# Float64 weights turned into float32 by shifting the scaled upper word: three VectorE and one ScalarE operation a piece

## The chip, the cores and the metric

The kernel runs on one core of a Trainium2 chip. The metric is the device time of one execution in microseconds, which includes the little that lies around the program's first and last instruction. Three runs of the kernel before the change took 480.67, 481.02 and 481.49 us.

The engines are called here as the profile calls them: PE (TensorE, the matrix engine), DVE (VectorE), ACT (ScalarE), POOL (GpSimd) and SP (SyncE, which issues all the DMAs of this kernel). Each engine takes its instructions strictly in the order in which the program gives them; an instruction that waits for another engine's semaphore holds up everything behind it on its own engine.

## The reference, cut to what matters

The first half is an mLSTM cell over 4 batches, 8 heads, 768 steps and a head width of 40; the second is a feed-forward block with an exact GELU over the 3072 rows that the cell gives.

```python
for t in range(S):
    m_new = np.maximum(f_gate[:, :, t] + m, i_gate[:, :, t])
    f_stab = np.exp(f_gate[:, :, t] + m - m_new)
    i_stab = np.exp(i_gate[:, :, t] - m_new)
    C = f_stab * C + i_stab * np.einsum('bhd,bhe->bhde', vt, kt)
    n = f_stab * n + i_stab * kt
    h_tilde = np.einsum('bhde,bhe->bhd', C, qt)
    y[:, :, t] = sigmoid(o_gate[:, :, t]) * h_tilde / np.maximum(np.abs(n . qt), 1.0)
x = y as (3072, 320)
h = x @ w_in                                    # 320 x 2048
g = 0.5 * h * (1.0 + erf(h / sqrt(2)))
out = g @ w_out                                 # 2048 x 320
```

All inputs are float32 but the two weights: `randn(...).astype(float32)` is multiplied by a numpy float64 scalar, and the products `w_in` and `w_out` are float64. [...]

## The kernel before, in words

**The cell.** The 768 steps are cut into six chunks of 128 (`NCH`), and each chunk into the four batches. A chunk's part of the cell is done with matrix products: for each batch the transposes of q and k (line 481), the scores (L507), the product of the scores with the decay weights on DVE (L510; the weights themselves are ACT's exponentials, L432, eight a batch), the products with the values (L621), the new state (L545, L550, ACT's copies at L560 for the first chunk), the division by the denominator on DVE (`finish`, L634 to L645) and the transposes of y (L656).

**The feed-forward block.** It follows chunk by chunk: `up_step` for the first chunk (L761, L767, GELU at L771), `first_down_steps` (L868), and for the five other chunks products of split parts (`up`, L816 and L827, GELU at L831) and seven products in place of eight (`down_steps`, L891).

**The weights.** They are fetched in 26 `pieces`: ten of 128 partitions by 512 weights for `w_in` (eight `w_in` and two `w_rest`), then 16 of 128 by 320 for `w_out`. `fetch` (L336) issues the DMAs of one piece from SP into one of four buffers `bits`, in which each weight's lower word `lo` lies ahead of its upper word `hi`, so that both are read at a stride of two words. `conv_one` and `conv_two` make the float32 from it:

* `conv_one`: DVE takes the exponent's bits out of `hi` (L357), ACT turns them into a power of two in two operations (L359, L360), and meanwhile DVE takes the mantissa's bits out of `hi` (L362) and adds the lower word (L364).
* `conv_two`: DVE puts the sign on the power of two (L371), multiplies the two parts (L374), and the next piece but three is fetched.

So a piece takes five operations of DVE and two of ACT. In `conv_one` nothing on DVE reads what ACT makes; the first reader of it is L371, in `conv_two`.

**The order.** Nothing is scheduled by a tool: `tc.manual_schedule()` keeps each engine's instructions in the order in which the Python code gives them, and the strings `FRONT` (first two chunks) and `DOWN` (the others) write this order down by hand, one letter a step. `K` is the next piece's `conv_one`, `J` the next piece's `conv_two`; w is the weights of the decay, s the scores, v the products with the values, y `finish`, x the transposes of y, c the carry of the state; capitals are the second chunk; `A` and `U` are steps of the first up product, `F` of the first down product. The letters `I` and `k` give a number of matrix products whose results are not read (L386, L215). The part of `FRONT` in which the first pieces lie is:

```python
O1 K L2 Q s0 O3 w2 q D k2 d P3 t1 w3 c0 L3 J v0 t2 K K y0 s1 I7 v1
I8 O2 J g1 L4 I5 c1 K I1 I2 y1 s2 x0 t3 B4 O4 B5 g2 J x1 s3 v2 c2 L5 y2 H T0 x2 G0 v3 g3 c3 K y3 M1 J L6 J A x3
```

Of the kernel before, what the change touches and what calls it, by code (L numbers as in the profile page):

```python
# [9 lines left out]
F32 = mybir.dt.float32  # L10
F32R = mybir.dt.float32r
BF16 = mybir.dt.bfloat16
U32 = mybir.dt.uint32
AF = mybir.ActivationFunctionType
OP = mybir.AluOpType

P = 128

I23 = 2.0 ** 23
PART = 1.0 - 2.0 ** -13  # L20
BASE = 1.0 + 2.0 ** -12

# [15 lines left out]
def kernel(  # L40
# [16 lines left out]
    nc = tc.nc  # L57
# [17 lines left out]
    WP = 512  # L75
# [3 lines left out]
    const = ctx.enter_context(tc.tile_pool(name="const", bufs=1))  # L79
    wts = ctx.enter_context(tc.tile_pool(name="wts", bufs=NW))  # L80
    raw = ctx.enter_context(tc.tile_pool(name="raw", bufs=2))
# [13 lines left out]

    w_out = const.tile([P, NF, DM], F32, name="w_out")
    ident = const.tile([P, P], F32, name="ident")
    e_hi = const.tile([P, 1], F32, name="e_hi")
    e_lo = const.tile([P, 1], F32, name="e_lo")
    first_x = raw.tile([P, NX + 1, TG], F32, name="first_x", tag="x", bufs=1)  # L100
    aT = const.tile([P, NCH, BH], F32, name="aT")
# [110 lines left out]
    def warm(n):  # L212
        cold = ps_h.tile([P, P], F32, name="cold", tag="h")
        for _ in range(n):
            nc.tensor.matmul(cold, w_out[:, 0, 0:P], w_out[:, 0, 0:P], start=True, stop=True, skip_group_check=True)  # L215

    nc.vector.memset(w_out[:, 0, 0:P], 0.5)
    warm(6)
    nc.vector.memset(e_hi, 1151.0 * I23)
    nc.vector.memset(e_lo, 255.0 * I23)  # L220

    nc.scalar.activation(out=m0[:, 1:2], in_=e_lo[0:BH], func=AF.Exp, scale=0.0)
# [92 lines left out]
    pieces = []  # L315
# [15 lines left out]
        return w_all[i // 4 * 5 + (2 if x == NX else x + (i % 4) // 2 * 3)]  # L331
    for f in range(NF):
        pieces.append(([w_src["out"][f * P:(f + 1) * P, :]], w_out[:, f, :]))
    bits, sig, pow2 = {}, {}, {}

    def fetch(i):  # L336
        if i >= len(pieces):
            return
        src, dst = pieces[i]
        n = sum(x.shape[0] * x.shape[1] for x in src) // (2 * P)  # L340
        bits[i] = raw.tile([P, WP, 2], U32, name="bits", tag="bits", bufs=NB)[:, 0:n, :]
        to = bits[i].rearrange("p n two -> p (n two)")
        row = col = 0
        for x in src:
            nc.sync.dma_start(out=to[row:row + x.shape[0], col:col + x.shape[1]], in_=x)
            row, col = (row + x.shape[0]) % P, col + (x.shape[1] if x.shape[0] == P else 0)

    def conv_one(i):

        if i < len(pieces):  # L350
            n = bits[i].shape[1]
            lo, hi = bits[i][:, :, 0], bits[i][:, :, 1]
            s = sig[i] = raw.tile([P, WP], F32, name="sig", tag="sig")[:, 0:n]
            p = pow2[i] = raw.tile([P, WP], F32, name="pow", tag="pow")[:, 0:n]
            su, pu = s.bitcast(U32), p.bitcast(U32)

            nc.vector.tensor_scalar(out=pu, in0=hi, scalar1=20, scalar2=0x7FF,  # L357
                                    op0=OP.logical_shift_right, op1=OP.bitwise_and)
            nc.scalar.activation(out=p, in_=pu, func=AF.Relu, scale=-I23, bias=e_hi)  # L359
            nc.scalar.activation(out=pu, in_=p, func=AF.Relu, scale=-1.0, bias=e_lo)  # L360

            nc.vector.tensor_scalar(out=su, in0=hi, scalar1=0xFFFFF, scalar2=0x100000,  # L362
                                    op0=OP.bitwise_and, op1=OP.bitwise_or)
            nc.vector.scalar_tensor_tensor(out=s, in0=lo, scalar=2.0 ** -32, in1=su, op0=OP.mult, op1=OP.add)  # L364

    def conv_two(i):

        if i < len(pieces):
            hi, p = bits.pop(i)[:, :, 1], pow2.pop(i)
            pu = p.bitcast(U32)  # L370
            nc.vector.scalar_tensor_tensor(out=pu, in0=hi, scalar=0x80000000, in1=pu,  # L371
                                           op0=OP.bitwise_and, op1=OP.bitwise_or)
            dst, s = pieces[i][1], sig.pop(i)
            nc.vector.scalar_tensor_tensor(out=dst, in0=s, scalar=2.0 ** -20, in1=p, op0=OP.mult, op1=OP.mult)  # L374
            fetch(i + NB)


# [14 lines left out]
    class Cell:  # L392
# [278 lines left out]
        def split_x(self, b):  # L671
            px, t = self.px.pop(b), slice(b * L, (b + 1) * L)
            hi = parts["x"][:, :, t]
            nc.vector.scalar_tensor_tensor(out=parts["x_lo"][:, :, t], in0=px, scalar=-1.0 / BASE, in1=hi, op0=OP.mult, op1=OP.add)
            nc.vector.tensor_tensor(out=parts["x_all"][:, :, t], in0=px, in1=hi, op=OP.subtract)
# [24 lines left out]
    def split_weight():  # L700
# [12 lines left out]
        w_lo.append(w_f(F32R, "w_in_lo"))  # L713
        nc.vector.scalar_tensor_tensor(out=w_lo[i], in0=w_hi[i], scalar=-BASE * 2.0 ** 12, in1=w, op0=OP.mult, op1=OP.add)

# [240 lines left out]
    def cell_steps(c, letters, before=None):  # L956
# [11 lines left out]
                 d=lambda: decays_last(0, 1), q=lambda: decays_last(1, NCH - 1), r=halves_out, p=halves_back,  # L968
                 A=in_turn(first_up_steps(0)), U=in_turn(first_up_steps(1)), F=in_turn(first_down_steps(first_g)),
                 K=in_turn(lambda i=i: conv_one(i) for i in n_pieces), H=products_begin,  # L970
                 J=in_turn(lambda i=i: conv_two(i) for i in n_pieces), Z=split_weight)
    steps |= cell_steps(0, "mwgtscvyx") | cell_steps(1, "MWGTSCVYXR")
    play(FRONT, steps)
# [40 lines left out]
```

## Time and profile before

| | |
|---|---|
| runs | 480.67, 481.02, 481.49 us (median 481.02) |
| profiled execution | span 479.0 us from the first to the last instruction; its own device time is not listed apart from the three runs, whose median is 2.0 us above the span |
| granted TensorE clock | 1.000 over the whole span |
| PE, DVE, ACT, POOL busy | 470.5, 351.5, 222.2, 70.4 us |
| conversion of the weights on DVE | 26 pieces between 14.2 and 125.6 us |
| the same on ACT | 26 pieces between 16.9 and 124.2 us |
| PE's last long wait | before 46.6 us; from there the chain that ended last runs on PE, with short exceptions, to the end |

How to read it: the profile gives each instruction's start and duration; an instruction that follows another on DVE or ACT without a wait may start some 0.1 us before the end of the one ahead of it. A matrix product of float32 stands in the trace as two instructions. The times in the text are microseconds from the first instruction. The releaser behind an arrow in square brackets is the instruction that ended an engine's idle time.

### The profile page before, as it was taken

How to read it: one execution, taken by the hardware profiler on the slowest of the kernel's cores; microseconds unless marked ns; L12 is line 12 of the kernel's file. 1: busy time of each engine (PE TensorE's matmuls, PEld its weight loads, DVE VectorE, ACT ScalarE, POOL GpSimd, SP SyncE). 2: the span in 40 equal slices, each digit the busy share in tenths (PEclk: the TensorE clock that was granted, in tenths of full speed). 3: DMA queues.
4: the chain of work that ended last, by engine and by line, in shares of the span. 5: the costliest groups of instructions: out<-in, count | busy, mean ns of one | idle time of the engine just before them, and what ended most of it. 6: DMA issues, size and time to landing. Idle time of an engine off the chain costs nothing.

```text
span 479.0 us, 11954 instructions
## 1 busy us (share of the span) xinstructions
PE 470.5 (98%) x4740; PEld 410.1 (86%) x4740; DVE 351.5 (73%) x762; ACT 222.2 (46%) x477; POOL 70.4 (15%) x104
## 2 busy tenths in 40 slices
PE   7899999999999999999999999999999999999997
PEld 7787888877777999977999977999977999977997
DVE  7899789798879999847589846589756599624321
ACT  6986999944532942112952113952113952112300
POOL 3001210000020225200324200324100222000000
PEclk9999999999999999999999999999999999999999
DMA  9998966289420367541356551367641350100001
GB/s 171 197 210 191 192 175 152 64 203 194 139 30 4 38 109 181 79 98 12 40 114 154 80 111 14 39 109 172 102 79 12 42 89 3 55 1 0 1 1 55
DMA packets 170423, 44.49 MB, mean 93 GB/s; under 512 B 156448, under 2 KB 163904, under 8 KB 170368
## 3 DMA queue, kind: packets, MB, share of 16 engines
q1 hardware_dynamic: 170368, 43.73, 46.4%
q8 instruction: 37, 0.61, 0.5%
q14 instruction: 18, 0.15, 0.1%
HBM read 39.58 MB, written 4.13 MB: 91 GB/s over the span
## 4 chain that ended last, share of the span: by engine, by line
PE 78%; issue 10%; DVE 7%; SPq 2%; DMA 1%; ACT 1%; POOL 0%; DVEq 0%; POOLq 0%
PE po L891 27%; PE pu L816 19%; PE po L868 7%; PE pu L761 5%; PE pu L827 5%; PE ph L621 4%; PE ps L523 2%; PE pu L767 1%; PE pf L589 1%; SPq L147 1%; PE px L656 1%; PE pf L578 1%; PE ps L507 1%; SPq L157 1%; PE pt L481 1%
## 5 line engine op out<-in xcount | busy, mean ns | idle before, releaser
L891 PE MATMUL po<-w_out,g 128*128 128x160 f32 x640 | 91.6, 301 | 0.0
L891 PEld LDWEIGHTS po<-w_out,g 128*128 128x128 f32 x640 | 87.7, 190 | 2.0 <-ACT g L831 1.8
L831 ACT ACTIVATE g<-pu 128x512 f32<-128x512 f32 x80 | 40.8, 614 | 52.9 <-PE pu L827 52.8
L891 PE MATMUL po<-w_sums,sums 128*128 128x160 f32 x320 | 47.7, 303 | 0.0
L891 PEld LDWEIGHTS po<-w_sums,sums 128*128 128x128 f32 x320 | 44.1, 190 | 0.7
L816 PE MATMUL pu<-x_hi,w_in_hi 128*128 128x512 f32 x160 | 41.7, 402 | 0.0
L666 ACT ACTIVATE x_hi<-px 128x384 fp32r<-128x384 f32 x20 | 9.8, 489 | 67.0 <-PE px L656 67.0
L816 PE MATMUL pu<-x_lo,w_in_lo 128*128 128x512 f32 x160 | 40.6, 395 | 0.0
L432 ACT ACTIVATE W<-W,aT 128x128 f32<-128x128 f32 x128 | 39.2, 388 | 0.1
L816 PEld LDWEIGHTS pu<-x_hi,w_in_hi 128*128 128x128 f32 x160 | 28.5, 188 | 9.3 <-ACT g L831 4.1
L748 DVE TENSOR_TENSOR sums<-g 128x512 f32<-128x512 f32 x20 | 13.8, 688 | 30.8 <-ACT g L831 30.8
L816 PEld LDWEIGHTS pu<-x_lo,w_in_lo 128*128 128x128 f32 x160 | 30.1, 188 | 7.2
L868 PE MATMUL po<-w_out,g 128*128 128x320 f32 x128 | 35.2, 433 | 0.0
L868 PEld LDWEIGHTS po<-w_out,g 128*128 128x128 f32 x128 | 24.0, 190 | 9.5
L831 ACT ACT_TABLE_LOAD x5 | 6.4, 1283 | 55.1 <-DMA blocks<-in_k_dram 27.6
L720 DVE TENSOR_TENSOR w_in_mid<-w_in_hi,w_in_lo 128x512 fp32r<-128x512 f32 x20 | 13.8, 688 | 24.4 <-PE pu L816 24.4
L816 PE MATMUL pu<-x_all,w_mid 128*128 128x512 f32 x80 | 31.6, 395 | 0.0
L816 PE MATMUL pu<-x_all,w_in_mid 128*128 128x512 f32 x80 | 31.6, 395 | 0.0
L444 POOL MEMSET g<- 32x1024 f32 x8 | 7.6, 945 | 150.1 <-ACT W L432 124.5
L406 POOL TENSOR_SCALAR_AFFINE_SELECT W<-W 128x1024 f32<-128x1024 f32 (+2 forms) x20 | 21.3, 1076 | 54.8 <-DMA W<-M_d 42.2
L904 DVE TENSOR_TENSOR o_sb<-po,o_sb 128x320 f32<-128x320 f32 (+1 forms) x27 | 12.5, 464 | 22.8 <-PE po L891 18.8
L761 PE MATMUL pu<-first_x,w_in 128*128 128x256 f32 x128 | 29.1, 382 | 0.1
(183 smaller groups left out, 915.6 us busy)
## 6 DMA issues: line engine op xcount, KB each, us to landing
W<-M_d SPq DMA_DIRECT2D x16, 512.0 KB, 5.6
bits<-in_moe_w_in_dram SPq DMA_DIRECT2D x20, 256.0 KB, 4.6
bits<-in_moe_w_out_dram SPq DMA_DIRECT2D x16, 320.0 KB, 3.3
ob<-in_o_gate_dram SPq DMA_DIRECT2D x24, 160.0 KB, 3.5
out_dram<-o_sb SPq DMA_DIRECT2D x24, 160.0 KB, 2.1
vb<-in_v_dram SPq DMA_DIRECT2D x14, 160.0 KB, 5.1
kb<-in_k_dram SPq DMA_DIRECT2D x14, 160.0 KB, 5.1
g<-M_d SPq DMA_DIRECT2D x4, 512.0 KB, 4.4
```

The source lines that it names most:

```text
L406: nc.gpsimd.affine_select(out=x, in_=x, compare_op=OP.is_ge, fill=1.0e30, base=base, pattern=[[0, H], [1, x.shape[2]]], channel_multiplier=-1)
L432: nc.scalar.activation(out=W[n][:, h, :], in_=src, func=AF.Exp, scale=-1.0, bias=aT[:, self.c, r:r + 1])
L621: nc.tensor.matmul(ph[r, h, :], Pm[:, h, r], vb[turn_of(n)][:, h, :], start=True, stop=True)
L720: nc.vector.tensor_tensor(out=w_mid[i], in0=w_hi[i], in1=w_lo[i], op=OP.add)
L748: nc.vector.tensor_tensor(out=s1, in0=a21, in1=a22, op=OP.add)
L761: nc.tensor.matmul(banks[-1][e][:, i - i0, :], in_tile(i, x)[:, e, i % 2 * P:(i % 2 + 1) * P], first_x[:, x, t0:t1], start=(x == 0 and i = ...
L816: nc.tensor.matmul(pus[i][e], w[k][:, e, i * P:(i + 1) * P], x[:, k, :], start=(n == 0 and k == 0), stop=False, skip_group_check=True)
L827: nc.tensor.matmul(pu[e], w[r, i // 2, i % 2 * P:(i % 2 + 1) * P], x[r, NX, :], start=False, stop=(n == 2), skip_group_check=True)
L831: nc.scalar.activation(out=g.t[:, HF * e + i, :], in_=pu[e], func=AF.Gelu, scale=4097.0)
L868: nc.tensor.matmul(po[b], g.t[:, f, b * L:(b + 1) * L], w_out[:, f, :], start=(f == 0), stop=(f == NF - 1))
L891: nc.tensor.matmul(bank[at][:, i, :], lhs(j, t), rhs(j), start=(first and i == 0 and j == 0), stop=(i == n - 1 and j == HF - 1), skip_grou ...
L904: nc.vector.tensor_tensor(out=to, in0=pb, in1=x, op=OP.add)
```

## The change

`conv_one` and `conv_two` make the float32 in another way. The upper word is read as if it were a float32, whose exponent has eight bits; a product with 2^-112 takes 112 off that exponent, that is 896 = 1023 - 127 off the eleven bits. Shifted to the left by three, the word then is a float32 without its sign and without its three lowest bits. These are the lower word times 2^-29, rounded, and the sign is the top bit of the upper word.

* ACT multiplies the upper words by 2^-112 in place (one operation in `conv_one`, strided in and out).
* DVE turns the lower words into the three bits in place (one operation in `conv_one`).
* DVE merges the sign of the upper word, as ACT left it, and the three bits into the weight's tile (the third operation of `conv_one`).
* DVE shifts the upper words by three and merges them with the weight's tile (the only operation of `conv_two`).

The tiles `sig`, `pow` and `e_hi` go. The order of the steps in `FRONT` stays, and so do the DMAs and their order.

```diff
+NEAR = 0.9374
-    e_hi = const.tile([P, 1], F32, name="e_hi")
-    nc.vector.memset(e_hi, 1151.0 * I23)
-    bits, sig, pow2 = {}, {}, {}
+    bits = {}
 def conv_one(i):
     if i < len(pieces):
-            n = bits[i].shape[1]
             lo, hi = bits[i][:, :, 0], bits[i][:, :, 1]
-            s = sig[i] = raw.tile([P, WP], F32, name="sig", tag="sig")[:, 0:n]
-            p = pow2[i] = raw.tile([P, WP], F32, name="pow", tag="pow")[:, 0:n]
-            su, pu = s.bitcast(U32), p.bitcast(U32)
-
-            nc.vector.tensor_scalar(out=pu, in0=hi, scalar1=20, scalar2=0x7FF,
-                                    op0=OP.logical_shift_right, op1=OP.bitwise_and)
-            nc.scalar.activation(out=p, in_=pu, func=AF.Relu, scale=-I23, bias=e_hi)
-            nc.scalar.activation(out=pu, in_=p, func=AF.Relu, scale=-1.0, bias=e_lo)
-
-            nc.vector.tensor_scalar(out=su, in0=hi, scalar1=0xFFFFF, scalar2=0x100000,
-                                    op0=OP.bitwise_and, op1=OP.bitwise_or)
-            nc.vector.scalar_tensor_tensor(out=s, in0=lo, scalar=2.0 ** -32, in1=su, op0=OP.mult, op1=OP.add)
+            dst = pieces[i][1].bitcast(U32)
+
+            nc.scalar.activation(out=hi.bitcast(F32), in_=hi.bitcast(F32), func=AF.Copy, scale=2.0 ** -112)
+            nc.vector.tensor_scalar(out=lo, in0=lo, scalar1=NEAR * 2.0 ** -29, scalar2=None, op0=OP.mult)
+            nc.vector.scalar_tensor_tensor(out=dst, in0=hi, scalar=0x80000000, in1=lo, op0=OP.bitwise_and, op1=OP.bitwise_or)

 def conv_two(i):
     if i < len(pieces):
-            hi, p = bits.pop(i)[:, :, 1], pow2.pop(i)
-            pu = p.bitcast(U32)
-            nc.vector.scalar_tensor_tensor(out=pu, in0=hi, scalar=0x80000000, in1=pu,
-                                           op0=OP.bitwise_and, op1=OP.bitwise_or)
-            dst, s = pieces[i][1], sig.pop(i)
-            nc.vector.scalar_tensor_tensor(out=dst, in0=s, scalar=2.0 ** -20, in1=p, op0=OP.mult, op1=OP.mult)
+            hi = bits.pop(i)[:, :, 1]
+            dst = pieces[i][1].bitcast(U32)
+            nc.vector.scalar_tensor_tensor(out=dst, in0=hi, scalar=3, in1=dst, op0=OP.logical_shift_left, op1=OP.bitwise_or)
             fetch(i + NB)
```

## The prediction

> **What bounds the kernel now.** I read the page first (engines, slices), then busy time by stretch, then the chain of waits, and last the time lines of DVE and ACT beside each other.
>
> ```profile
> span 479.0 us, 11954 instructions
> PE 470.5 (98%) x4740; PEld 410.1 (86%) x4740; DVE 351.5 (73%) x762; ACT 222.2 (46%) x477; POOL 70.4 (15%) x104
> ...
> PE   7899999999999999999999999999999999999997
> ```
>
> Busy time by stretch (start:end, length, then PE, PEld, DVE, ACT, POOL, granted clock, DMA share, GB/s):
>
> ```profile
> 12.00:24.00 12.00, 10.76 (x137) 8.51 (x135) 10.39 (x28) 11.69 (x40) 0.00 (x0) 1.00 1.03 197
> 24.00:36.00 12.00, 11.38 (x159) 10.00 (x158) 10.98 (x26) 9.66 (x17) 0.00 (x0) 1.00 1.03 210
> 36.00:48.00 12.00, 11.19 (x131) 9.16 (x128) 11.59 (x28) 8.44 (x17) 2.39 (x2) 1.00 0.85 190
> 48.00:93.60 45.60, 45.60 (x508) 39.53 (x506) 37.22 (x85) 43.73 (x83) 4.86 (x4) 1.00 0.65 150
> ```
>
> From 48 us PE has no idle time; the chain runs on it from 46.59 to the end. Only what moves the start of that run, or opens a hole in it, moves the time. Before 48, PE, DVE and ACT take turns: PE is idle 1.24 + 0.62 + 0.81 = 2.67 us in the three stretches. So work taken off DVE can gain some 2.7 us at most, while a late product moves everything behind it. The pieces' place, DVE first, then ACT:
>
> ```profile
> 14.24 0.41 DVE L357 TENSOR_SCALAR pow<-bits 128x512 uint32<-128x512 uint32 x1
> ...
> 15.02 0.69 DVE L364 SCALAR_TENSOR_TENSOR sig<-bits,sig 128x512 f32<-128x512 uint32 x1
> 15.63 0.25 DVE L234 COPY ewT<-pg 128x96 f32<-128x96 f32 x1
> ...
> 21.67 0.42 DVE L357 TENSOR_SCALAR pow<-bits 128x512 uint32<-128x512 uint32 x1
> ...
> 24.57 0.49 DVE L634 TENSOR_TENSOR ob<-ph,ob 128x320 f32<-128x320 f32 x1
> ...
> 29.21 0.42 DVE L357 TENSOR_SCALAR pow<-bits 128x512 uint32<-128x512 uint32 x1
> ```
>
> ```profile
> 14.89 2.09 ACT L432 ACTIVATE W<-pm,aT 128x128 f32<-128x128 f32 x8
> 16.89 0.71 ACT L359 ACTIVATE pow<-pow,e_hi 128x512 f32<-128x512 uint32 x1
> ...
> 24.84 0.73 ACT L359 ACTIVATE pow<-pow,e_hi 128x512 f32<-128x512 uint32 x1
> ...
> 31.25 0.72 ACT L359 ACTIVATE pow<-pow,e_hi 128x512 f32<-128x512 uint32 x1
> ```
>
> The reader should lay these two side by side. DVE starts piece 0 at 14.24, ACT at 16.89; piece 1 at 21.67 and 24.84; piece 3 at 29.21 and 31.25; further down the same lists piece 4 at 39.67 and 41.59, piece 6 at 47.85 and 52.11, piece 7 at 54.57 and 59.63, piece 11 at 73.96 and 77.46. ACT lags because eight exponentials, table loads or copies of PE's results stand ahead of its part. Before, nobody pays: DVE reads ACT's result only in the later step `conv_two` (5.1 us of waits in all, 3.0 of them one).
>
> **The change part by part.** *DVE work.* A piece loses one two-constant operation (L362, 0.42 us at 512 columns, 0.32 at 320) and one with two tensors (0.69, 0.49): 10 x 1.11 + 16 x 0.81 = 24.1 us. What is left is priced by its like: the scaling of the lower words by L357 (0.42, 0.32; uint32 and stride two as there, but its output is strided and its arithmetic not bitwise, so up to L364's 0.69 and 0.49), both merges by L371 (0.69, 0.49).
>
> *ACT work.* Two operations (0.72 + 0.72; 0.56 + 0.56) become one. It is a Copy with a constant scale and no bias tile like L712 (median 0.62 at 512), so I take 0.62, and 0.47 at 320 (L438, 0.46, is near); the bounds are 0.59 (L484) and, as no row shows stride two in place on ACT, the 1.44 of both operations that it replaces; DVE's L364 reads at stride two at the 0.69 of L374's dense operands, so I stay near the dense price. That saves 8 + 10 = 18 us of ACT. L712's Copy stands between exponentials and GELU without a table load, and the built program has 32 loads as before.
>
> *The new wait.* The third operation of `conv_one`, the merge of the sign, reads the upper word that ACT has just scaled. In the built program it waits on ACT's semaphore. So DVE now stops inside `conv_one` until ACT has come to the piece; queued behind it on DVE are `finish`, the score products (L510), the values' weighting and the state update, for which PE and then ACT wait. I walked the queues with the profile's durations, each instruction at the later of its queue and its inputs:
>
> 1. Piece 0: ACT is free at 16.90 (its exponentials wait for nothing new) and done at 17.52. DVE is ready at 14.66, so it stalls 2.9; the merge ends at 18.25 and L234 starts at 18.17, not 15.63: +2.54. L510 had idled 0.58 for PE at 16.66, so it is +1.88, and PE, which had waited 0.41 for DVE's decays (L282), is +1.74.
> 2. Piece 1: `conv_two` of piece 0 is 0.72 shorter; DVE starts at 21.67 + 1.74 - 0.72 = 22.7 and is ready at 23.1. ACT's own queue moved with PE: 24.84 + 1.74, done at 27.24. Stall 4.2. Piece 2 follows without one; L634 starts at 28.96, not 24.57: +4.39, and PE's values product, which waited for L510, goes from 27.61 to 32.00.
> 3. Piece 3: ACT's copies of the state (L560, 30.64 + 4.39) stand ahead, ACT is done at 36.16, DVE stalls 3.0; L634 30.61 becomes 36.81. Idle time on PE and one shorter `conv_two` take back 0.7: the first up product, 40.80, is +5.49.
> 4. Piece 4: ACT done at 47.60, stall 2.1; then two `conv_two` save 1.4. The second up product, 46.59, is +5.74.
> 5. Pieces 5 to 9: stalls of 0.6, 3.25, 2.5, 2.4, one of none; PE has enough queued, nothing is added.
> 6. Pieces 10 and 11: ACT is behind its GELU and tables; stalls of 3.3 and 1.0 make the state update (L565, 76.05) late, and L545 at 78.06 waits 1.15 more: +6.89. After that the walk finds no new hole in PE's run: the pieces of `w_out` stay ahead of the products that read them.
>
> *SP.* `conv_two` still issues the fetch four pieces on, and SP already stands 30.6 us before such issues; these and the loads behind them slide with the rest. A piece lands in 4.6 us and has over ten (piece 8: issued 44.5, used 62.9), so I cost it at nothing; without that cover one late piece costs its landing. POOL gets no work. The tiles `sig` and `pow` go, and with them waits of L720's tiles past 129 us, where PE has no idle time before them: nothing. One memset of 0.06 us goes: nothing.
>
> *Sum.* The walk gives 479.0 + 6.9 = 485.9 for this execution, and the median of the runs stands 2.0 above its span: 487.9. In the walk L639 and L645 keep their 0.75 and 0.99 us at 42.10 and 42.88, beside two operations of POOL (0.49 and 0.23 elsewhere); moved away from them the path loses 1.0. I take half: 487.4.
>
> [...] The row: in the first 14 pieces ACT starts its part 0.5 to 5.2 us after DVE. [...] With the scaling on DVE (10 x 0.42 + 16 x 0.32 = 9.3 us of the 24.1 given back) the wait would go, and the sum would be that of the first rival below.
>
> **The rivals.** *The wait is covered, and the time falls.* If ACT reached its part before DVE reaches the merge, 1.1 us less DVE work in a piece would bring the first up products forward. The chain of waits passes through conversion at 23.1, 39.8 and 43.9, which speaks for it. PE's idle time bounds it by 2.7; half of that gives 479.7. It decides where ACT's start in a piece lies no later than DVE's; the lists have it later in all of the first 14 pieces, by 0.5 to 5.2 us, which speaks against it.
>
> *PE's covered run takes it all up, no change.* Step 5 shows stalls that cost nothing. But steps 1 to 4 lie where PE already waits on DVE and ACT. Time 481.
>
> *The operations are dearer too.* In the walk ACT's operation at 0.74 (L359's longest) adds 0.7 and DVE's scaling at 0.69 adds 0.3: 488.9. ACT at 1.44 adds 5.5: 493.4.
>
> **How the numbers follow.** The forecast, stalls with like-priced operations, 0.84; dearer operations 0.07; covered wait 0.06; no change 0.03. Low end: step 6 left out (-1.15), the whole 1.0 of POOL's neighbourhood and another 0.8 from shorter DMA issues once they start later: 487.9 - 3.0, rounded down for other such neighbourhoods, 484.5. High end 490.5: the 488.9, and a third of the way from there to 493.4. Some 0.2% (1 us) is what a measurement of this kernel can tell from no change. Faster 0.06, same 0.03, slower 0.91.
>
> **What would show it.** Right: the merge at line 355 has idle time on DVE before it, ended by ACT's operation at 353, some 28 us over all pieces and over 2 us at pieces 0, 1, 3 and 4; DVE's conversion falls by about 24 us and yet the up product that started at 46.59 starts at 51 to 53; from there the two traces run in parallel. Wrong: no such idle time; ACT's operation off 0.6; PE's run beginning earlier than 46; or a shift that shrinks again behind 50 us, which would mean that PE's run has idle time that I can't see.

## The result, and the profile after

Four runs of the changed kernel took 491.95 to 496.16 us, median 493.0, against 480.67 to 481.56 (median 481.25) for four of the kernel before: a ratio of 1.0255 [1.0212, 1.0298]. The prediction said 487.4, from 484.5 to 490.5. The direction was right; the loss is 11.8 us where 6.4 had been forecast. The profiled run is the one of 496.16 us, with a span of 494.0.

From the page of the changed kernel, the span, the busy times, and the slices of PE and of its granted clock (40 slices of 12.35 us, in tenths; 9 is 90% or more):

```profile
span 494.0 us, 11935 instructions
...
PE 478.5 (97%) x4740; PEld 416.6 (84%) x4740; DVE 327.3 (66%) x709; ACT 204.6 (41%) x451; POOL 71.3 (14%) x104
...
PE   8777999999999999999999999999999999999997
...
PEclk9778899999999999999999999999999999999999
```

DVE has 24.2 us less to do than before (351.5) and ACT 17.6 less (222.2), as forecast. But PE, with the same 4740 instructions, is busy for 8.0 us longer than before (470.5), and the last row says why: between 12 and 62 us its clock was not the full one.

Busy time by stretch after the change (start:end, length, then PE, PEld, DVE, ACT, POOL, granted clock, DMA share, GB/s):

```profile
12.00:24.00 12.00, 9.21 (x71) 7.22 (x71) 7.02 (x20) 8.05 (x26) 0.00 (x0) 0.81 1.01 206
24.00:36.00 12.00, 8.67 (x120) 7.42 (x118) 5.85 (x14) 6.61 (x17) 0.00 (x0) 0.78 0.32 74
36.00:48.00 12.00, 9.93 (x118) 8.50 (x116) 5.67 (x14) 3.67 (x8) 0.47 (x1) 0.84 0.82 213
48.00:60.00 12.00, 10.97 (x106) 9.40 (x107) 7.49 (x20) 6.62 (x14) 1.93 (x2) 0.86 0.22 48
60.00:93.60 33.60, 32.31 (x337) 27.54 (x338) 18.60 (x42) 28.80 (x57) 4.63 (x4) 1.00 0.76 180
```

From 12 to 24 us PE carries out 71 instructions where it carried out 137; DVE falls from 10.39 us of work to 7.02 and ACT from 11.69 to 8.05. All three engines have become idler at once, so they wait for each other.

The time line of DVE after the change, at the conversion's first merge (now L355) and `finish` (L622, L634 before):

```profile
13.86 0.41 DVE L354 TENSOR_SCALAR bits<-bits 128x512 uint32<-128x512 uint32 x1
17.19 0.69 DVE L355 SCALAR_TENSOR_TENSOR w_in<-bits 128x512 uint32<-128x512 uint32 x1 [2.91 <-ACT bits L353]
...
23.10 0.42 DVE L354 TENSOR_SCALAR bits<-bits 128x512 uint32<-128x512 uint32 x1
29.49 0.69 DVE L355 SCALAR_TENSOR_TENSOR w_in<-bits 128x512 uint32<-128x512 uint32 x1 [5.97 <-ACT bits L353]
...
31.74 0.49 DVE L622 TENSOR_TENSOR ob<-ph,ob 128x320 f32<-128x320 f32 x1
...
41.39 0.69 DVE L355 SCALAR_TENSOR_TENSOR w_in<-bits 128x512 uint32<-128x512 uint32 x1 [5.32 <-ACT bits L353]
42.00 0.49 DVE L622 TENSOR_TENSOR ob<-ph,ob 128x320 f32<-128x320 f32 x1
...
55.57 0.69 DVE L355 SCALAR_TENSOR_TENSOR w_in<-bits 128x512 uint32<-128x512 uint32 x1 [3.74 <-ACT bits L353]
```

The same stretch on ACT, whose part of the conversion is now L353:

```profile
14.51 2.09 ACT L420 ACTIVATE W<-pm,aT 128x128 f32<-128x128 f32 x8
16.51 0.65 ACT L353 ACTIVATE bits<-bits 128x512 f32<-128x512 f32 x1
...
24.30 2.18 ACT L420 ACTIVATE W<-pm,aT 128x128 f32<-128x128 f32 x8 [0.27 <-PE pm L417]
26.32 0.61 ACT L548 COPY state<-pf 64x164 f32<-64x164 f32 x2
...
28.78 1.25 ACT L353 ACTIVATE bits<-bits 128x512 f32<-128x512 f32 x2
...
40.05 0.59 ACT L548 COPY state<-pf 64x164 f32<-64x164 f32 x2 [8.24 <-PE pf L533]
40.67 0.69 ACT L353 ACTIVATE bits<-bits 128x512 f32<-128x512 f32 x1
```

Read the two together. Piece 0 is the forecast itself: DVE is ready at 14.3 and stands 2.91 us because ACT is at its exponentials. Piece 1 should have cost 4.2 us and costs 5.97, piece 3 costs 5.32 for 3.0, piece 4 3.74 for 2.1. Over all pieces the first merge waits 36.4 us for ACT, in 13 of the 26. At piece 3 the circle closes: DVE waits for ACT, ACT has waited 8.24 us for PE's state product, and PE has waited for DVE, as its own time line after the change shows:

```profile
21.46 1.09 PE L469 MATMUL pt<-ident,kb 128*128 128x128 f32 x4
...
34.19 0.44 PE L609 MATMUL ph<-vb,W 128*64 128x41 f32 x4 [3.17 <-DVE W L498]
...
36.44 2.50 PE L374 MATMUL pf<-ident 128*128 128x128 f32 x10
...
54.07 3.72 PE L749 MATMUL pu<-first_x,w_in 128*128 128x256 f32 x16
```

The four instructions at 21.46 take 1.09 us, the four of the same kind at 27.07 take 0.66. The group at 36.44 takes 2.50; the like group of ten takes 1.38 in the kernel `raw_sign` below, at 27.95. So PE's products are slow just where PE, ACT and DVE hang on one another. Stretches of 3.41 us of the changed kernel, cut where its granted clock changes, with the columns of the table above:

```profile
15.93:19.34 3.41, 2.05 (x20) 1.15 (x16) 2.15 (x5) 3.22 (x12) 0.00 (x0) 1.00 0.89 153
19.34:22.75 3.41, 2.80 (x13) 2.77 (x14) 1.89 (x9) 0.15 (x1) 0.00 (x0) 0.50 1.01 254
22.75:26.17 3.42, 3.42 (x36) 2.56 (x34) 0.77 (x2) 2.89 (x10) 0.00 (x0) 0.50 0.93 175
...
29.58:33.00 3.42, 1.43 (x13) 1.24 (x12) 2.79 (x8) 2.20 (x3) 0.00 (x0) 1.00 0.03 7
33.00:36.41 3.41, 2.07 (x32) 1.87 (x32) 3.04 (x7) 0.00 (x0) 0.00 (x0) 0.50 0.01 3
36.41:39.82 3.41, 3.41 (x28) 3.15 (x26) 0.00 (x0) 0.00 (x0) 0.00 (x0) 0.50 1.00 237
...
43.23:46.65 3.42, 2.15 (x33) 1.70 (x33) 2.51 (x6) 1.38 (x4) 0.00 (x0) 1.00 0.79 211
46.65:50.06 3.41, 1.78 (x46) 1.61 (x43) 3.31 (x8) 0.26 (x1) 2.40 (x2) 1.00 0.81 212
50.06:53.48 3.42, 3.42 (x42) 3.09 (x41) 1.74 (x5) 2.71 (x7) 0.00 (x0) 0.50 0.19 35
```

Three times PE is busy for only 1.43 to 2.05 of 3.4 us, and each time a granted clock of 0.50 follows: from 19.34 to 26.17, 33.00 to 39.82 and 50.06 to 53.48, together 17.07 us. PE is busy for 15.12 of these; by an estimate from that clock and the longer groups above (1.09 for 0.66, 2.50 for 1.38) up to 15.12 / 2 = 7.6 us of them are lost. The first up product starts 54.07 - 40.80 = 13.27 us later than before. Of these the prediction had 5.5. Another 0.9 is an operation of DVE that runs beside POOL's two (from 47.53, 2.40 us):

```profile
47.57 1.40 DVE L482 TENSOR_TENSOR vw<-vb,ewT 128x328 f32<-128x328 f32 x1
```

The same operation took 0.49 us before (L494, at 36.74), and PE's state product at 49.03 waits 1.63 us for it where it had waited 0.72. The 6.9 us that are left lie within the 7.6 of the half clock. From there the two traces run almost in parallel: the third up product starts at 67.21 instead of 53.88 (+13.33), a wait of 1.03 us for DVE's state update comes in at 92.70, and the span ends 15.0 later.

### The profile page after: what moved, and what is told of

Read it like the earlier page. It is cut to its first block, busy times and chain, and to the rows that moved or that the text cites. A ratio compares the mean times of both kernels' runs of the same rounds, so it can differ in the third digit from the quotient of the medians.

```text
span 494.0 us, 11935 instructions
## 1 busy us (share of the span) xinstructions
PE 478.5 (97%) x4740; PEld 416.6 (84%) x4740; DVE 327.3 (66%) x709; ACT 204.6 (41%) x451; POOL 71.3 (14%) x104
## 4 chain that ended last, share of the span: by engine, by line
PE 75%; issue 10%; DVE 5%; ACT 4%; DMA 4%; SPq 2%; POOL 1%; POOLq 0%; DVEq 0%; ACTq 0%
PE po L879 27%; PE pu L804 18%; PE po L856 7%; PE pu L815 5%; PE pu L749 4%; PE ph L609 4%; PE ps L511 2%; PE px L644 1%; ACT W L420 1%; SPq L157 1%; PE pf L577 1%; PE pu L755 1%; PE pf L566 1%; DMA W<-M_d 1%; DMA g<-M_d 1%
```

## The experiments

The theory: the first merge stands in `conv_one` and reads ACT's result, DVE waits, everything queued on DVE is late, PE idles and then runs at half clock. The rivals: the new operations are dearer than thought; a semaphore between DVE and ACT, or the tile changed in place, costs wherever it stands; SP's fetches come later and cost; the loss is spread over all 26 pieces. "The walk" is the walk of the queues that the prediction made, at full clock, with an experiment's edit made in it. All ratios are to the kernel before on the same chip. `raw_sign`, `wait_first`, `wait_rest` and `fill` ran on one chip (19 runs of before, median 481.06), `later`, `before_wait`, `dve_scale` and `lean` on another (29 runs, 480.75). Diffs are against the changed kernel unless said otherwise, and show the lines that matter.

### raw_sign: the same operations without the wait

```diff
-            nc.scalar.activation(out=hi.bitcast(F32), in_=hi.bitcast(F32), func=AF.Copy, scale=2.0 ** -112)
+            s = scaled[i] = raw.tile([P, WP], F32, name="sig", tag="sig")[:, 0:bits[i].shape[1]]
+            nc.scalar.activation(out=s, in_=hi.bitcast(F32), func=AF.Copy, scale=2.0 ** -112)
 def conv_two(i):
-            hi = bits.pop(i)[:, :, 1]
-            dst = pieces[i][1].bitcast(U32)
+            bits.pop(i)
+            hi, dst = scaled.pop(i).bitcast(U32), pieces[i][1].bitcast(U32)
```

> The change with one thing different: ACT writes its product into a tile of its own (128x512 float32, as the old sig), and the merge in conv_one takes the sign from the upper word as it was fetched, whose top bit is the same. Counts, order and shapes of the operations stay; only the merge's wait for ACT goes. Theory W (that wait holds DVE, PE starves, its clock is halved): the walk of the queues with the durations of before gives 1.0 us less than before, so 479.5 to 481.5 in the median, granted clock 1.00, no idle time before the merge. Rival O (the new operations are dearer than the old): 490 to 494, as the change. Rival S (later fetches on SP): 490 to 494 too, as SP's order is the same.

Measured: 479.85 us, ratio 0.9968 [0.995, 0.9986]; span 477.7, granted clock 1.000. The time line of DVE in `raw_sign` (the scaling is L355 here, the first merge L356):

```profile
14.29 0.41 DVE L355 TENSOR_SCALAR bits<-bits 128x512 uint32<-128x512 uint32 x1
14.74 0.69 DVE L356 SCALAR_TENSOR_TENSOR w_in<-bits 128x512 uint32<-128x512 uint32 x1
```

No arrow: the merge follows at once, where it stood 2.91 us. The first up product starts at 40.19, 0.6 us before the kernel before, and the whole loss of 11.8 us is gone, with ACT's result in a tile of its own and the merge reading the word as fetched. The new arithmetic is not what costs; it gains 1.2 us (the walk: 1.0) of the 2.7 that PE's idle time allowed. What ACT's operation costs was settled already by the trace of the changed kernel: 0.65 to 0.72 us at 512 columns and 0.48 to 0.52 at 320 (means 0.68 and 0.50), taken as 0.62 and 0.47.

### later: the same five instructions, one of them moved

```diff
 def conv_one(i):
-            nc.vector.scalar_tensor_tensor(out=dst, in0=hi, scalar=0x80000000, in1=lo, op0=OP.bitwise_and, op1=OP.bitwise_or)
 def conv_two(i):
+            nc.vector.scalar_tensor_tensor(out=dst, in0=hi, scalar=0x80000000, in1=lo, op0=OP.bitwise_and, op1=OP.bitwise_or)
             nc.vector.scalar_tensor_tensor(out=dst, in0=hi, scalar=3, in1=dst, op0=OP.logical_shift_left, op1=OP.bitwise_or)
```

> The change with both merges in conv_two: conv_one is ACT's product and DVE's scaling of the lower word, and DVE first reads ACT's result in conv_two, some microseconds of other work later, as in the kernel before. The same five instructions a piece as the change, one moved. Theory W: the walk gives 0.9 us less than before, 479.5 to 481.5, clock 1.00. Rival O or a cost of the operations: 490 to 494.

Measured: 479.68 us, 0.9969 [0.9949, 0.9988]; first up product at 40.22. Here the merge reads ACT's result just as in the changed kernel, only later in the queue, and the whole loss is gone again. So neither the semaphore nor the in-place tile costs anything in itself; what costs is where the wait stands in DVE's queue. This run also answers the rival of the fetches: in `raw_sign` nothing reads the fetched words after `conv_one`, so their buffer is free for SP earlier, but in `later` both merges read them in `conv_two`, as late as in the changed kernel.

### before_wait: the wait alone, in the kernel before

```diff
 def conv_one(i):   # against the kernel before: L371 from the head of conv_two to the end of conv_one
+            nc.vector.scalar_tensor_tensor(out=pu, in0=hi, scalar=0x80000000, in1=pu,
+                                           op0=OP.bitwise_and, op1=OP.bitwise_or)
 def conv_two(i):
-            nc.vector.scalar_tensor_tensor(out=pu, in0=hi, scalar=0x80000000, in1=pu,
-                                           op0=OP.bitwise_and, op1=OP.bitwise_or)
```

> The kernel before with one operation moved: the sign's merge (L371), which reads what ACT makes, stands at the end of conv_one and not at the head of conv_two. Same operations, counts and shapes as before. Theory W: DVE now waits inside conv_one for two ACT operations, with none of its work taken off; the walk with the durations of before gives 17.0 us more, and the clock falls when PE idles: 497 to 508. Rival O (the change is slower because its operations are): this kernel has the old ones, so 481 to 483.

Measured: 503.2 us, 1.0432 [1.0394, 1.0471]; first up product at 56.31, mean clock 0.979. From the waits of DVE in `before_wait` (engine, line, releaser: total us, times, longest):

```profile
DVE pow L365 <- ACT pow L360: 35.4, 26, 5.5
```

The old arithmetic with its own reader of ACT's result moved up loses 22.4 us (the walk, at full clock: 17.0; the mean clock of 0.979 over 501.7 us is worth up to 10.5 more). With `raw_sign` and `later` this shows the cause from both sides: take the wait out of `conv_one` and the loss goes, put it in and it comes, whatever the arithmetic.

### wait_first and wait_rest: which pieces count

Both are `raw_sign`, with ACT's operation back in place in some pieces, so that the merge waits there. The diff is against `raw_sign`:

```diff
-            s = scaled[i] = raw.tile([P, WP], F32, name="sig", tag="sig")[:, 0:bits[i].shape[1]]
+            s = scaled[i] = (raw.tile([P, WP], F32, name="sig", tag="sig")[:, 0:bits[i].shape[1]] if i >= 5
+                             else hi.bitcast(F32))
```

This is `wait_first`; `wait_rest` has `i < 5` there.

> As the change in pieces 0 to 4 (merge waits for ACT), sign from the fetched word in pieces 5 to 25 (no wait). Theory W: the damage is done while PE has no work queued, so pieces 0 to 4 alone cost 5.9 us by the walk and the halved clock on top: 487 to 494. Rival E (every stall costs its share, 20 of some 36 us of stalls here): half of the change's 11.8 us, 486 to 488, with nothing between this kernel and the change explained by place.

> The complement: no wait in pieces 0 to 4, the change's wait in pieces 5 to 25. Theory W: PE has enough queued from 41 us on, so the 22 us of stalls cost 0.5 us by the walk: 480 to 482.5, clock 1.00. Rival E (every stall costs its share): 485 to 488. Rival O (dearer operations): 490 or more.

Measured: `wait_first` 490.31 us, 1.0189 [1.0151, 1.0227], with 15.0 us of waits for ACT in 4 of the first five pieces; `wait_rest` 482.69, 1.0022 [1.0001, 1.0044], with 18.6 us of them in 9 of the later pieces. More waiting, and less than a third of the cost: against `raw_sign` 2.8 us instead of 10.5. So waits at pieces 0 to 4, where PE has little queued, make most of the loss; late pieces, the spread-out rival, are worth little. `wait_rest` came out 0.2 us above the upper end of what was expected. Part of that is no matter of the waits: in its profiled run (483.99 us) the clock was halved from 15.46 to 18.88, before any piece that waits, which is worth up to 1.7 us; the eight of its ten runs with a mean clock of 0.999 or 1.000 have a median of 482.25. The rest says that late waits cost more than the 0.5 us that the walk gave them.

### fill: keep PE busy through the waits

32 more products whose results are not read, at the places where PE idles:

```diff
 FRONT:
-    I2 O0 g0 L0 P0 L1 E k1 t0 P1 P2 k7 w0 N k2 w1 O1 K L2 Q s0 O3 w2 q D k2 d P3 t1 w3 c0 L3 J v0 t2 K K y0 s1 I7 v1
-    I8 O2 J g1 L4 I5 c1 K I1 I2 y1 s2 x0 t3 B4 O4 B5 g2 J x1 s3 v2 c2 L5 y2 H T0 x2 G0 v3 g3 c3 K y3 M1 J L6 J A x3
+    I2 O0 g0 L0 P0 L1 E k1 t0 P1 P2 k7 w0 N k2 w1 O1 K L2 Q s0 O3 w2 k4 q k4 D k2 d P3 t1 w3 c0 L3 J v0 t2 K K y0 s1 I21 v1
+    I8 O2 J g1 L4 I5 c1 K I1 I2 y1 s2 x0 t3 B4 O4 B5 g2 J I6 x1 s3 v2 I4 c2 L5 y2 H T0 x2 G0 v3 g3 c3 K y3 M1 J L6 J A x3
```

> The change with 32 more unread 128x128 products on PE at four places where its trace shows PE waiting for DVE (8 around the turning of the decays at 17 to 20 us, 14 ahead of the values product at 31, 6 and 4 ahead of a transpose and a state product at 43 to 49). The wait of DVE for ACT stays as it is. Theory W with the clock as its second half: the stalls stay, but PE is not idle in them, the granted clock stays at 1.00 or loses one stretch, and the time falls to what the walk gives for the stalls alone, 486 to 489. Rival C (the halved clock is not caused by PE's idle time): stays at 491 to 496 with a clock of 0.98 to 0.99. If the extra products cost more than they fill: above 494.

Measured: 489.35 us, 1.0177 [1.0128, 1.0225]; the clock was 1.000 in all four runs. Two stretches of the changed kernel:

```profile
17.00:20.40 3.40, 1.42 (x8) 0.91 (x7) 2.96 (x9) 2.15 (x9) 0.00 (x0) 0.84 0.80 139
...
30.60:34.00 3.40, 0.41 (x4) 0.22 (x2) 2.81 (x8) 1.20 (x2) 0.00 (x0) 0.85 0.01 2
```

and the same stretches of `fill`:

```profile
17.00:20.40 3.40, 3.23 (x27) 2.66 (x24) 2.60 (x7) 2.69 (x10) 0.00 (x0) 1.00 0.85 140
...
30.60:34.00 3.40, 3.00 (x47) 2.65 (x47) 3.33 (x8) 0.00 (x0) 0.00 (x0) 1.00 0.00 0
```

PE has more to do, and the kernel is 3.7 us shorter in the median; the longest of its four runs (491.70) is shorter than the shortest of the changed kernel (491.95). DVE still waits for ACT, 29.2 us in 12 pieces, but no longer than 4.1 at once. From DVE's time line in `fill`, pieces 0, 1 and 3:

```profile
17.73 0.70 DVE L355 SCALAR_TENSOR_TENSOR w_in<-bits 128x512 uint32<-128x512 uint32 x1 [2.93 <-ACT bits L353]
...
27.45 0.69 DVE L355 SCALAR_TENSOR_TENSOR w_in<-bits 128x512 uint32<-128x512 uint32 x1 [4.09 <-ACT bits L353]
...
37.10 0.69 DVE L355 SCALAR_TENSOR_TENSOR w_in<-bits 128x512 uint32<-128x512 uint32 x1 [3.06 <-ACT bits L353]
```

The walk had 2.9, 4.2 and 3.0 there. This shows the clock as a cost of its own beside the waits, and the longer stalls of the changed kernel as a consequence of the half clock. The time came out 0.35 us above the expected 486 to 489, and its span (487.1 in two of the runs) is 1.2 above the 485.9 of the walk; the added products are not free, and how much of the 1.2 is theirs was not measured.

### dve_scale: the multiplication on DVE

```diff
-            nc.scalar.activation(out=hi.bitcast(F32), in_=hi.bitcast(F32), func=AF.Copy, scale=2.0 ** -112)
+            nc.vector.tensor_scalar(out=hi.bitcast(F32), in0=hi.bitcast(F32), scalar1=2.0 ** -112, scalar2=None, op0=OP.mult)
```

> The change with the product with 2^-112 on DVE (0.42 us at 512 columns) and not on ACT: four DVE operations a piece in place of three, none on ACT, no wait for another engine. Theory W: 9.3 us more DVE work than the change, but no wait: the walk gives 0.7 us less than before, 480 to 482. If DVE's count of operations decides: slower than the change, 493 or more.

Measured: 480.86 us, 0.9989 [0.997, 1.0008], not to be told from no change. Here one more operation a piece on DVE removes the wait, and it is 12 us cheaper than the same operation on ACT. Its profiled run, too, had half clock for a stretch: from 12 to 24 us its granted clock was 0.86, which is some 3.4 us at 0.50, though no wait for ACT is left in its conversion.

### lean: what is left to gain

`raw_sign` without nine of the unread products (`I8` and `I1` are overwritten by a later `I` before they are used, so no product is issued for them):

```diff
 FRONT:
-    I2 O0 g0 L0 P0 L1 E k1 t0 P1 P2 k7 w0 N k2 w1 O1 K L2 Q s0 O3 w2 q D k2 d P3 t1 w3 c0 L3 J v0 t2 K K y0 s1 I7 v1
-    I8 O2 J g1 L4 I5 c1 K I1 I2 y1 s2 x0 t3 B4 O4 B5 g2 J x1 s3 v2 c2 L5 y2 H T0 x2 G0 v3 g3 c3 K y3 M1 J L6 J A x3
+    I2 O0 g0 L0 P0 L1 E k1 t0 P1 P2 k7 w0 N k2 w1 O1 K L2 Q s0 O3 w2 q D k2 d P3 t1 w3 c0 L3 J v0 t2 K K y0 s1 I5 v1
+    O2 J g1 L4 c1 K y1 s2 x0 t3 B4 O4 B5 g2 J x1 s3 v2 c2 L5 y2 H T0 x2 G0 v3 g3 c3 K y3 M1 J L6 J A x3
```

> The kernel with the sign from the fetched word (479.85 us) and nine of its unread 128x128 products on PE taken out: two ahead of the values product at 26.9 us, all five ahead of the state product at 29.3 and all two ahead of the scores at 30.5, 0.22 us each, 2.0 us. In that kernel's trace DVE's and ACT's results stand ready before these products end. Theory W: PE's long run begins up to 2.0 us earlier, 478 to 479.5, if the granted clock stays at 1.00. If the missing products let the clock fall for a stretch of 3.4 to 6.8 us: 481 to 483.5.

Measured: 479.65 us, 0.9965 [0.9943, 0.9988], from 478.22 to 482.62: no better than `raw_sign` (479.85), and above the 478 to 479.5 expected at full clock. PE's work fell by 2.1 us (467.6 against 469.7), and the first up product starts only 0.33 earlier. On DVE's time line in `lean` stands what is late next:

```profile
38.21 0.50 DVE L483 TENSOR_TENSOR vw<-vb,ewT 128x328 f32<-128x328 f32 x1 [2.46 <-DMA vb<-in_v_dram]
```

and on PE's:

```profile
39.27 0.67 PE L534 MATMUL pf<-vw,qk 128*64 128x41 f32 x16 [2.05 <-DVE vw L483]
```

The values' load for a later batch lands at 38.2, having been issued by SP at 32.46, behind a mask load that held SP for 2.15 us. In `raw_sign` the same operation starts at 38.24 without a wait. So the next limit of this stretch is that load; moving it was not tried. Four of the twelve runs of `lean` had a mean clock of 0.988 or 0.996, against one of the ten of `raw_sign`; but `raw_sign` ran on the other chip, and on the chip of `lean` the kernel before, with all its unread products, had such a clock in 11 of 29 runs, so it is not shown that the missing products did this.

| kernel | median us | ratio | first up product | waits of the first merge for ACT |
|---|---|---|---|---|
| lean | 479.65 | 0.9965 | 39.86 | none |
| later | 479.68 | 0.9969 | 40.22 | none in `conv_one` |
| raw_sign | 479.85 | 0.9968 | 40.19 | none |
| dve_scale | 480.86 | 0.9989 | 41.21 | none |
| wait_rest | 482.69 | 1.0022 | 42.24 | 18.6 us, pieces 5 on |
| fill | 489.35 | 1.0177 | 47.90 | 29.2 us |
| wait_first | 490.31 | 1.0189 | 50.21 | 15.0 us, pieces 0 to 4 |
| the changed kernel | 493.0 | 1.0255 | 54.07 | 36.4 us |
| before_wait | 503.2 | 1.0432 | 56.31 | 35.4 us |

The first up products of `wait_rest` and `dve_scale` are from executions that had half clock for 3.4 us ahead of them. Three versions, `lean`, `later` and `raw_sign`, beat both kernels, by 0.3% over the kernel before; among runs with a mean clock of 0.999 or more it is 0.2%, as some runs of the kernel before have half clock for a stretch themselves. Among themselves they are not told apart.

## Why the prediction was wrong where it was

* **What bounds the kernel, and the work.** Right. DVE's relief of 24.2 us (24.1 forecast) bought nothing that the path could use: without the wait it is worth 1.2 us.
* **Steps 1 to 4, the wait.** Right in place, kind and order; piece 0 to the tenth (2.9 and 2.91 us). From piece 1 on the stalls are larger (5.97, 5.32, 3.74 instead of 4.2, 3.0, 2.1), because ACT, for which DVE waits, waits for PE, and PE was at half clock from 19.34. At full clock, in `fill`, the stalls at pieces 1 and 3 were 4.09 and 3.06.
* **Step 5 and step 6.** Step 6 is right: it forecast 1.15 us of new idle time at the state product, and the changed kernel has 1.03 there, at 92.70. Step 5 was put at nothing and costs a little: the third up product waits for DVE and starts 8.04 us after the second, against 7.62 in `raw_sign`. `wait_rest` puts steps 5 and 6 together at 2.8 us in the median, 2.5 in the runs at full clock.
* **The operations.** Right: 0.69 and 0.49 for both merges, 0.41 to 0.43 in the first pieces and a median of 0.33 over all for the scaling, with a longest of 0.91. ACT's operation is about a tenth dearer than taken at 512 columns.
* **The neighbourhood of POOL.** Half of 1.0 us was taken off. The two operations that took 0.75 and 0.99 beside POOL's do take 0.49 and 0.23 now, at 57.21 and 57.73. But POOL's two operations now run at 47.53, beside the values' weighting at 47.57, which takes 1.40 instead of 0.49 and stands ahead of the first up product. So in this run the cost moved and did not go, and nothing should have been taken off. The 0.8 for shorter DMA issues in the low end was an estimate. Three of SP's pairs of issues for `bits` did get shorter, 1.05, 0.82 and 0.82 us (at 18.59, 23.25 and 35.39) where they had taken 1.40, 2.42 and 1.96 (at 20.03, 22.64 and 28.18); what that gave in time was not measured.
* **The sum: here it failed.** It priced every step of PE at the durations of before, all of them at full clock. It had no term for the clock, although it put some 6 us of new idle time on PE. That term measures up to 7.6 us in the profiled run and 3.7 in the median by `fill`, whose added products are not free. Taking (1 - mean clock) x span, the most that half clock can have cost, off the four runs' spans, 494.0 at 0.982, 490.2 and 489.8 at 0.993, 491.7 at 0.986, leaves 485.1, 486.8, 486.4 and 484.8: a mean of 485.8, where the walk had 485.9, and `fill` at full clock has 487.1. So the walk was right to about 1 us, and the missing term is nearly the whole of the 5.6 us by which 487.4 missed 493.0. That 485.8 and 485.9 are so close is in part luck: 485.8 has the most taken off that half clock can have cost, and the walk left out the 0.4 of step 5 and a tenth of ACT's operation.
* **The high end.** It was drawn from a rival, dearer operations, that the rows already spoke against, and not from the resource that the forecast itself was going to disturb. With the half clock in it, by an estimate from the spells of these runs one of 3.41 us for each of the four long stalls, 4 x 1.7 = 6.8 us, the high end would have been near 494.
* **What would have shown it.** The merge's idle time (28 us forecast, 36.4 measured) and DVE's 24 us are there. The second up product was to start at 51 to 53 and starts at 59.17 (45.90 before, with its last wait over at 46.59): this line is the one that fails, and it points to the stretch before it.

One row bears on the missing term. After the stretch of the changed kernel from 15.93 to 19.34, with PE busy for 2.05 of 3.41 us and no single wait of PE in it longer than 1.05, the granted clock was 0.50. So PE need not be wholly idle ahead of such a clock.

## What to carry to other kernels

Before an operation is moved or fused, ask which engine's result each instruction now reads, and what is queued behind it: here DVE stopped for ACT's result a step early, and with it all that was behind it in its queue (493.0 us with the merge in `conv_one`, 479.68 with it in `conv_two`), and 24 us of saved work did not pay for that. Where a forecast puts idle time on PE in a stretch in which it is already not full, add a term for half clock (here two to five times 3.4 us of it in a run, by the mean clocks of 0.993 to 0.982, at up to 1.7 us each), and put it into the range. The cure is mostly cheap: read the untouched operand (`raw_sign`, 479.85 us), or move the waiting instruction to where its input is long done (`later`, 479.68).

## What was not expected of the hardware

In the changed kernel the half clock comes in spells of 3.41 or 6.83 us; in `before_wait` the granted clock from 36 to 48 us was 0.57, which is some 10.3 us at 0.50. The three spells of the changed kernel start 13.66 and 17.06 us apart, which is four and five times 3.41. They follow stretches in which PE was busy for 1.43, 1.78 and 2.05 of 3.4 us; yet the stretch from 43.23 to 46.65, with 2.15, was not followed by one. Busy time by stretch in `wait_rest`, before and in its halved spell:

```profile
12.06:15.46 3.40, 2.59 (x25) 1.77 (x24) 3.29 (x9) 3.15 (x11) 0.00 (x0) 1.00 0.88 208
15.46:18.88 3.42, 3.42 (x27) 2.92 (x27) 1.64 (x4) 2.48 (x10) 0.00 (x0) 0.50 0.93 156
```

and the same stretch in the kernel before, where no spell followed:

```profile
12.06:15.46 3.40, 2.59 (x25) 1.77 (x23) 3.29 (x9) 3.16 (x11) 0.00 (x0) 1.00 1.02 239
```

The same 25 instructions with the same 2.59 us of PE, and two outcomes. The busy share alone does not decide: the 2.59 us in `wait_rest` were followed by half clock, and the 2.15 of the changed kernel from 43.23 to 46.65 were not. What does decide is not shown by these runs. The kernel before has such spells too, by its mean clocks: of its 19 runs beside `raw_sign` three had a mean clock of 0.996, among them the two longest, 484.07 and 484.21 us, and of its 29 runs on the other chip eleven had 0.996 or 0.989. At a span of 482 a mean clock of 0.996 is worth up to 1.9 us.
